# Nonlinear part of two chunks in joined operations, with one scale for w_out, in a kernel of sigmoid attention and an MLP

## The chip, the cores and the metric

The kernel runs on one core of a Trainium2 chip. The metric is the device time of one execution in microseconds. An engine's name stands for its queue too: instructions of one engine run in the order in which they stand, and an instruction that waits holds up all that stand behind it.

## The reference

Attention with a sigmoid in place of the softmax, over 8 batches of 12 heads, 448 positions and 64 values a head, then an MLP whose nonlinear function is made of three pieces.

```python
scores = scale * np.matmul(q, k.transpose(0, 1, 3, 2)) - np.log(S)
attn = 1.0 / (1.0 + np.exp(-scores))
x = np.matmul(attn, v)                      # (8, 12, 448, 64) -> (3584, 768)
h = x @ w_in                                # (3584, 2048)
g = np.where(h >= 1, h, np.where(h <= -1, 0.0, (h + 1) ** 2 / 4))
return g @ w_out                            # (3584, 768)
```

Inputs and result are float32. The kernel works with float16 pairs: a number is scaled by a power of two and split in a high and a low half, and a product of two numbers is three matmuls (high by high, high by low, low by high).

## The kernel before

**Batches.** The work goes batch by batch (b = 0 to 7), each with 448 columns. The attention of batch b + 1 (`scores`, `weigh`, `av`: lines 410 to 530) runs between the MLP matmuls of batch b. It comes in pieces: score matmuls into `psc` (L438, L429), a sigmoid on ScalarE (L474), its high half on ScalarE (L482) and low half on VectorE (L483), then matmuls with v into `pav` (L520).

**The MLP of a batch.** Its first half makes h, 2048 rows in 16 chunks of 128, and from it g, as float16 halves in `ghl[:, f, half, :]` for chunk f. Its second half, the *downs* (`down`, L784), makes 6 output tiles, each from 48 matmuls over the 16 chunks, and scales and stores them.

**Batches 0 and 1** make h chunk by chunk (`up`, L748) and apply the nonlinear part to each (`bend`, L753 to L765). w_out is split in two groups of 8 chunks, each with a scale of its own (`wo.scale[0]`, `wo.scale[1]`), since the first group is needed in batch 0 before all of w_out has been seen.

**Batches 2 to 7** work at half size (`up_blocks`, L697): h of chunks i and i + 8 together, a *pair*, is made from 7 products of half-size blocks (9 matmuls of 224 columns each, L714), with weights combined beforehand (`mix`) and stored as `blocks`. The products j = 0 to 6 of pair i add up in four quarters of PSUM, in two banks `hold[i, 0]` and `hold[i, 2]`. VectorE and ScalarE put the quarters together: `u2` and `u3` are partial sums, and the four quarters of the result are a copy of quarter 0 (L732) and three sums (L723), in `hf` (chunk i) and `hg` (chunk i + 8). Three PSUM banks are shared by products and downs, so a bank's sums must be read before products of the next pair but one can start. After the last product both chunks get their nonlinear part:

```python
nc.scalar.activation(g, h, AF.Relu, bias=hr, scale=ihr)                                              # L761
nc.vector.scalar_tensor_tensor(out=g, in0=g, scalar=rt, in1=g, op0=ALU.min, op1=ALU.mult)            # L762
nc.vector.scalar_tensor_tensor(out=g, in0=h, scalar=ihs, in1=g, op0=ALU.mult, op1=ALU.max)           # L763
latest["g"] = nc.scalar.activation(hi, g, AF.Copy)                                                   # L764
(nc.gpsimd if f % GPOOL else nc.vector).tensor_tensor(out=ghl[:, f, 1, :], in0=g, in1=hi, op=ALU.subtract)  # L765
```

`GPOOL` is 1, so L765 runs on VectorE. The scales (`hr`, `ihr`, `rt`, `ihs`) are one number per batch and group, worked out by one-column operations on VectorE (`small`, L578) in `common_scales`. There the groups' different w_out scales are met by square roots (`roots`, `wo.root`, `wo.iroot`): each group's g gets a scale that makes up for that of its w_out, so that the downs can add up both groups.

**Order.** A scheduler places the instructions of all engines by priorities and by its own estimate of times; the sums of quarters have a raised priority (`Q_PRIO`). Loads and stores are issued by SyncE in the order of the program. GpSimd splits q, k and v of later head pairs (L373 to L375) and copies corner blocks (L454).

Of the kernel before, what the change touches and what calls it, by code (L numbers as in the profile page):

```python
# [71 lines left out]
def sigmoid_attention_mlp(ctx: ExitStack, tc: tile.TileContext, first_qvk, qkv, w_in, w_out, out_t):  # L72
# [525 lines left out]
    def inverse(tag, s):  # L598

        return small(tag, s, -1.0, ALU.mult, float(2 * 127 * EXP_ONE), ALU.add, ints=True)  # L600
# [5 lines left out]
        up_sc[b, k] = sc = up_scales(*largest(inv_x, k), k)  # L606
        down_sc[b, k] = lambda: small("od%d" % k, inverse("ig%d" % k, sc[4]), wo.inv[k], ALU.mult)

    def roots():

        for k in range(2):
            for t, lst, n in ((wo.scale[k], wo.root, "root"), (wo.inv[k], wo.iroot, "iroot")):
                r = const.tile([P, 1], F32, name=n + str(k))
                nc.vector.tensor_scalar(
                    out=r.bitcast(I32), in0=t.bitcast(I32), scalar1=0.5, scalar2=float(127 * EXP_ONE // 2),
                    op0=ALU.mult, op1=ALU.add,
                )
                lst.append(r)
# [80 lines left out]
    def up_blocks(b, i, j):  # L699

        n = (b - SB) * (NFC // 2) + i
        if j % 2 == 0 and j < 4:
# [8 lines left out]
        out, w = quarter(q), sets[n % 3]
        for c in range(HC):
            for wh, xh in ((0, 0), (0, 1), (1, 0)):
                nc.tensor.matmul(  # L714
                    out, w[:, wt, wh, c * P : (c + 1) * P], xc[:, xt, c, xh, :],
                    start=j in (0, 2) and c + wh + xh == 0, stop=c == HC - 1 and wh == 1,
                    skip_group_check=True,
                )
# [4 lines left out]
        add = lambda out, q, other: nc.vector.tensor_tensor(out=out, in0=quarter(q), in1=other, op=ALU.add)  # L723
        with tc.high_priority(offset=Q_PRIO):
            if j == 1:
                nc.scalar.activation(u2, quarter(0), AF.Copy)
# [28 lines left out]
    def bend(b, f, h):  # L755

        ihr, hr, rt, ihs, _ = up_sc[b, int(f >= NA)]
        g = tmp_p.tile([P, S], F32, tag="tmp", name="g")
        hi = ghl[:, f, 0, :]

        nc.scalar.activation(g, h, AF.Relu, bias=hr, scale=ihr)  # L761
        nc.vector.scalar_tensor_tensor(out=g, in0=g, scalar=rt, in1=g, op0=ALU.min, op1=ALU.mult)  # L762
        nc.vector.scalar_tensor_tensor(out=g, in0=h, scalar=ihs, in1=g, op0=ALU.mult, op1=ALU.max)  # L763
        latest["g"] = nc.scalar.activation(hi, g, AF.Copy)  # L764
        (nc.gpsimd if f % GPOOL else nc.vector).tensor_tensor(out=ghl[:, f, 1, :], in0=g, in1=hi, op=ALU.subtract)  # L765
# [124 lines left out]
    for u, unit in enumerate(units):  # L890
# [12 lines left out]
        if wo.at < NA + 1:  # L903
            convert(wo, min(NA + 1, (u + 1) * (NA + 1) // WO_A))
            if wo.at == NA + 1:
                wo.find_scale()
                split_at = 0
        elif wo.at < NFC + 1:
            convert(wo, min(NFC + 1, NA + 1 + (u + 1 - WO_A) * (NFC - NA) // (WO_B - WO_A)))
            if wo.at == NFC + 1:  # L910
                wo.find_scale()
                roots()
        if len(wo.scale):
            while split_at < min(NA, 2 * (u + 1 - WO_A)):
# [85 lines left out]
```

## Time and profile before

| what | us |
|---|---|
| median of 3 runs (1158.22, 1158.45, 2932.11) | 1158.45 |
| profiled execution, its own time | 1152.84 |
| its span, first to last instruction | 1151.1 |
| idle TensorE in the span (1151.1 - 1120.0) | 31.1 |
| length of one half-size batch (499.75 to 636.43 us) | 136.7 |

The run of 2932.11 us is no typical one; the median stands on the other two. Batches 2 to 5 repeat with the same length. In a row of groups the columns are line, engine, operation, output and inputs, shape and count, then busy time and mean time of one, then idle time before it and what ended that. In a row of the timeline the first two numbers are start and length in us, and the brackets hold the idle time before and its releaser. In a row of waits stand the total in us, how often, and the longest.

### The profile page before, as it was taken

How to read it: one execution, taken by the hardware profiler on the slowest of the kernel's cores; microseconds unless marked ns; L12 is line 12 of the kernel's file. 1: busy time of each engine (PE TensorE's matmuls, PEld its weight loads, DVE VectorE, ACT ScalarE, POOL GpSimd, SP SyncE). 2: the span in 40 equal slices, each digit the busy share in tenths (PEclk: the TensorE clock that was granted, in tenths of full speed). 3: DMA queues.
4: the chain of work that ended last, by engine and by line, in shares of the span. 5: the costliest groups of instructions: out<-in, count | busy, mean ns of one | idle time of the engine just before them, and what ended most of it. 6: DMA issues, size and time to landing. Idle time of an engine off the chain costs nothing.

```text
span 1151.1 us, 20032 instructions
## 1 busy us (share of the span) xinstructions
PE 1120.0 (97%) x7914; PEld 660.7 (57%) x7914; DVE 831.4 (72%) x1730; ACT 721.2 (63%) x1199; POOL 291.3 (25%) x367
## 2 busy tenths in 40 slices
PE   8899999999889999999999999999999998999998
PEld 2234434444446775478645776457754677548954
DVE  6988977789985996469945798368974599646820
ACT  6978988679765785457754687347773476423410
POOL 0000000003442344323623353515344234110000
PEclk9999999999999999999999999999999999999999
DMA  9933432153453653125421345114532054103300
GB/s 367 394 107 132 162 124 74 35 192 119 161 182 120 220 193 108 49 91 193 157 105 50 130 170 195 50 50 169 186 140 69 22 189 173 65 17 123 136 24 25
DMA packets 32511, 151.64 MB, mean 132 GB/s; under 512 B 3488, under 2 KB 14240, under 8 KB 26272
## 3 DMA queue, kind: packets, MB, share of 16 engines
q1 hardware_dynamic: 30688, 140.92, 33.8%
q10 hardware_dynamic: 1728, 9.44, 2.2%
q8 instruction: 62, 1.02, 0.4%
q14 instruction: 33, 0.27, 0.1%
HBM read 126.94 MB, written 23.40 MB: 131 GB/s over the span
## 4 chain that ended last, share of the span: by engine, by line
PE 67%; DVE 20%; ACT 7%; issue 2%; DMA 2%; SPq 0%; DVEq 0%; ACTq 0%
PE po L784 35%; PE ph L714 11%; PE ph L748 8%; PE pav L520 6%; DVE ahl L483 5%; PE psc L438 4%; DVE g L762 4%; DVE g L763 3%; DVE xhl L723 2%; ACT ahl L482 2%; ACT psc L474 2%; DVE ghl L765 1%; PE psc L429 1%; DMA blocks<-mixs 1%; ACT ghl L764 1%
## 5 line engine op out<-in xcount | busy, mean ns | idle before, releaser
L784 PE MATMUL po<-ghl,w_out_sb 128*128 128x448 f16 x2304 | 447.7, 354 | 2.9 <-DVE g L763 2.9
L784 PEld LDWEIGHTS <-w_out_sb 128*128 128x128 f16 x2304 | 222.5, 98 | 220.4 <-issue 19.5
L714 PE MATMUL ph<-w_in_sb 128*128 128x224 f16 x3024 | 303.7, 259 | 10.6 <-DVE xhl L723 10.5
L714 PEld LDWEIGHTS <-w_in_sb 128*128 128x128 f16 x3024 | 284.4, 98 | 37.7 <-issue 36.4
L483 DVE SCALAR_TENSOR_TENSOR ahl<-psc,ahl 128x896 f16<-128x896 f32 (+1 forms) x170 | 153.0, 900 | 113.2 <-ACT ahl L482 111.4
L474 ACT ACTIVATE psc<-psc,nls,sqk 128x896 f32<-128x896 f32 (+1 forms) x136 | 130.3, 971 | 116.6 <-PE psc L438 113.4
L373 POOL TENSOR_SCALAR raw<-raw,qkv_s 128x448 f32<-128x448 f32 (+1 forms) x93 | 68.6, 752 | 427.6 <-DVE qkv_i L137 368.5
L482 ACT ACTIVATE ahl<-psc 128x896 f16<-128x896 f32 (+1 forms) x170 | 128.0, 762 | 23.3 <-DVE ahl L483 21.8
L748 PE MATMUL ph<-xhl,w_in_sb 128*128 128x448 f16 x576 | 112.8, 353 | 0.0
L761 ACT ACTIVATE g<-xhl,hr,ihr 128x448 f32<-128x448 f32 x96 | 67.8, 753 | 56.4 <-DVE xhl L723 56.2
L764 ACT ACTIVATE ghl<-g 128x448 f16<-128x448 f32 x128 | 73.2, 572 | 46.5 <-DVE g L763 46.4
L765 DVE TENSOR_TENSOR ghl<-g,ghl 128x448 f16<-128x448 f32 x128 | 91.1, 718 | 11.9 <-ACT ghl L764 11.0
L723 DVE TENSOR_TENSOR xhl<-ph,xhl 128x224 f32<-128x224 f32 x240 | 86.3, 382 | 16.9 <-PE ph L714 10.6
L762 DVE SCALAR_TENSOR_TENSOR g<-g,rk 128x448 f32<-128x448 f32 x112 | 83.9, 764 | 14.8 <-ACT g L761 14.3
L438 PE MATMUL psc<-hl 64*128 64x448 f16 x756 | 91.3, 352 | 0.3 <-ACT a L471 0.3
L748 PEld LDWEIGHTS <-w_in_sb 128*128 128x128 f16 x576 | 54.6, 98 | 59.9 <-issue 9.7
L520 PE MATMUL pav<-ahl,v 128*64 128x448 f16 x748 | 83.7, 357 | 0.0
L375 POOL TENSOR_TENSOR hl<-raw,hl 128x448 f16<-128x448 f32 x62 | 72.5, 1190 | 0.0
L797 DVE TENSOR_SCALAR o<-po,od 128x448 f32<-128x448 f32 x42 | 28.5, 679 | 59.0 <-PE po L784 58.8
L763 DVE SCALAR_TENSOR_TENSOR g<-xhl,ihs,g 128x448 f32<-128x448 f32 x96 | 69.3, 739 | 0.1
L337 ACT ACTIVATE dump<-raw 128x448 f16<-128x448 f32 (+1 forms) x105 | 61.5, 586 | 2.7 <-DVE mb L154 1.3
L454 POOL COPY w_in_sb<-hl 64x128 f16<-64x128 f16 x68 | 27.8, 409 | 129.3 <-DVE hl L369 127.4
(149 smaller groups left out, 1080.0 us busy)
## 6 DMA issues: line engine op xcount, KB each, us to landing
w_in_sb<-blocks SPq DMA_DIRECT2D x48, 1344.0 KB, 6.0
raw<-qkv SPq DMA_DIRECT2D x34, 704.0 KB, 4.2
w_out_sb<-w_in SPq DMA_DIRECT2D x16, 768.0 KB, 11.1
out_t<-o SPq DMA_DIRECT2D x48, 224.0 KB, 1.9
blocks<-mixs SPq DMA_DIRECT2D x8, 768.0 KB, 3.3
w_out_sb<-w_out ACTq DMA_DIRECT2D x6, 768.0 KB, 4.9
raww<-w_out ACTq DMA_DIRECT2D x6, 768.0 KB, 5.3
blocks<-mixp SPq DMA_DIRECT2D x8, 576.0 KB, 3.4
```

The source lines that it names most:

```text
L438: run(lambda: nc.tensor.matmul(out, hl[rows, 1, kh, w], hl[rows, 0, qh, :], start=t == 0, stop=t == 2))
L474: nc.scalar.activation(a, a, AF.Sigmoid, bias=nls, scale=sqk)
L482: nc.scalar.activation(hi, x, AF.Copy, scale=ATT)
L483: made.setdefault(i, []).append(nc.vector.scalar_tensor_tensor(out=lo, in0=x, scalar=ATT, in1=hi, op0=ALU.mult, op1=ALU.subtract))
L520: run(lambda: once(nc.tensor.matmul(pav[j * D : (j + 1) * D, :S], *terms[j][t], start=c == 0 and t == 0, stop=mid and t == len(terms[j]) - ...
L714: nc.tensor.matmul(out, w[:, wt, wh, c * P : (c + 1) * P], xc[:, xt, c, xh, :], start=j in (0, 2) and c + wh + xh == 0, stop=c == HC - 1 a ...
L723: add = lambda out, q, other: nc.vector.tensor_tensor(out=out, in0=quarter(q), in1=other, op=ALU.add)
L748: nc.tensor.matmul(ph[:, :S], w_in_sb[:, f, wh, c * P : (c + 1) * P], xhl[:, c, xh, :], start=c == 0 and wh + xh == 0, stop=c == NCC - 1 a ...
L762: nc.vector.scalar_tensor_tensor(out=g, in0=g, scalar=rt, in1=g, op0=ALU.min, op1=ALU.mult)
L763: nc.vector.scalar_tensor_tensor(out=g, in0=h, scalar=ihs, in1=g, op0=ALU.mult, op1=ALU.max)
L765: (nc.gpsimd if f % GPOOL else nc.vector).tensor_tensor(out=ghl[:, f, 1, :], in0=g, in1=hi, op=ALU.subtract)
L784: nc.tensor.matmul(po[:, :S], w_out_sb[:, f, wh, m * P : (m + 1) * P], ghl[:, f, gh, :], start=f == lo and wh + gh == 0, stop=f == hi - 1 ...
```

## The change

In batches 2 to 7 the nonlinear part of a pair is one chain of five operations over both chunks, 2 x 448 columns (`bends`), where there were two chains of five operations of 448. Its intermediate g no longer has a tile of its own: it lies, as float32, in the place in `ghl` where the halves of chunks i and i + 8 will stand. Two of the three sums of quarters (quarter 3 and quarter 2, each plus u2) become one operation of 2 x 224 columns.

One operation has one scale, so both groups of w_out must have one too. Once the second group's scale is known, `join_scales` takes the smaller of both; the second group is split with that, and the first group, split already, is multiplied by the ratio in batch 1 (`rescale`, eight GpSimd operations of 1536 columns, one for each chunk). `roots` goes, and `common_scales` gets shorter. Batches 0 and 1 keep `bend`.

```diff
-    def roots():
...
+    def join_scales():
+        for lst, n, op in ((wo.scale, "wos", ALU.min), (wo.inv, "woi", ALU.max)):
+            t = const.tile([P, 1], F32, name=n)
+            nc.vector.tensor_scalar(out=t, in0=lst[0], scalar1=lst[1], scalar2=None, op0=op)
+            lst[1] = t
+        wo.ratio = const.tile([P, 1], F32, name="wor")
+        nc.vector.tensor_scalar(out=wo.ratio, in0=wo.scale[1], scalar1=wo.inv[0], scalar2=None, op0=ALU.mult)
+
+    def rescale(f):
+        w = w_out_sb[:, f].rearrange("p h n -> p (h n)")
+        nc.gpsimd.tensor_scalar(out=w, in0=w, scalar1=wo.ratio, scalar2=1.0, op0=ALU.mult, op1=ALU.mult)
+
     def common_scales(b, inv_x, ih=None):
         big = [largest(inv_x, k) for k in range(2)]
-        q = [small("q%d" % k, big[k][1], wo.root[k], ALU.mult) for k in range(2)]
-        q = small("qm", q[0], q[1], ALU.min)
+        rt = small("rk", big[0][1], big[1][1], ALU.min)
         for k in range(2):
-            up_sc[b, k] = up_scales(ih or big[k][0], small("rk%d" % k, q, wo.iroot[k], ALU.mult), k)
-        od = inverse("od", small("qq", q, q, ALU.mult))
+            if k and ih:
+                up_sc[b, 1] = up_sc[b, 0]
+            else:
+                up_sc[b, k] = up_scales(ih or big[k][0], rt, k)
+        od = small("od", inverse("ig", up_sc[b, 0][4]), wo.inv[1], ALU.mult)
...
-                add(hg[:, :HN], 2, u2)
-                add(hf[:, HN:], 3, u2)
+                both = hold[i, 2].rearrange("p (k n) -> p k n", k=2)[:, ::-1, :HN]
+                nc.vector.tensor_tensor(
+                    out=h[:, HN : 3 * HN].rearrange("p (k n) -> p k n", k=2), in0=both,
+                    in1=u2.unsqueeze(1).to_broadcast([P, 2, HN]), op=ALU.add,
+                )
         if j == 6:
-            bend(b, i + NFC // 2, hg)
-            bend(b, i, hf)
+            bends(b, i, h.rearrange("p (k n) -> p k n", k=2))
...
+    def bends(b, i, h):
+        ihr, hr, rt, ihs, _ = up_sc[b, 0]
+        g = ghl.rearrange("p f h n -> p f (h n)").bitcast(F32)[:, i :: NFC // 2, :]
+        hi, lo = (ghl[:, i :: NFC // 2, t, :] for t in range(2))
+        nc.scalar.activation(g, h, AF.Relu, bias=hr, scale=ihr)
+        nc.vector.scalar_tensor_tensor(out=g, in0=g, scalar=rt, in1=g, op0=ALU.min, op1=ALU.mult)
+        nc.vector.scalar_tensor_tensor(out=h, in0=h, scalar=ihs, in1=g, op0=ALU.mult, op1=ALU.max)
+        nc.scalar.activation(hi, h, AF.Copy)
+        nc.vector.tensor_tensor(out=lo, in0=h, in1=hi, op=ALU.subtract)
...
         if b == 1:
             mix_scales()
+            for f in range(NA):
+                rescale(f)
```

The scheduler places the instructions anew. In the changed kernel the lines are L719 for the products, L728 and L740 for the sums, L780 to L784 for the five operations of `bends`, L803 for the downs and L621 for the rescale.

VectorE at the end of the products of the last batch, before: the last sums, then the operations of both chunks (`rk_11674` and `rk_11664`, `ihs_11678` and `ihs_11668` are the scales of the two groups).

```order
L723 TENSOR_TENSOR xhl<-ph,xhl 128x224
L762 SCALAR_TENSOR_TENSOR g<-g,rk_11664 128x448
L763 SCALAR_TENSOR_TENSOR g<-xhl,ihs_11678,g 128x448
L763 SCALAR_TENSOR_TENSOR g<-xhl,ihs_11668,g 128x448
L765 TENSOR_TENSOR ghl<-g,ghl 128x448 x2
L723 TENSOR_TENSOR xhl<-ph,xhl 128x224 x2
L762 SCALAR_TENSOR_TENSOR g<-g,rk_11674 128x448
L762 SCALAR_TENSOR_TENSOR g<-g,rk_11664 128x448
```

And with the change: from the two sums of the last pair (L728) on, L781 and L782 are those of pair 6, L740 the joined sum of pair 7, L784 the difference of pair 6, and the last row the first operation of pair 7.

```order
L728 TENSOR_TENSOR xhl<-ph,xhl 128x224 x2
L781 SCALAR_TENSOR_TENSOR ghl<-ghl,rk 128x2x448
L782 SCALAR_TENSOR_TENSOR xhl<-xhl,ihs_11260,ghl 128x896
L740 TENSOR_TENSOR xhl<-ph,xhl 128x448
L784 TENSOR_TENSOR ghl<-xhl,ghl 128x2x448
L781 SCALAR_TENSOR_TENSOR ghl<-ghl,rk 128x2x448
```

Before, the differences of pair 6 (L765) stood ahead of the last sums; now that of pair 6 (L784) stands behind the last sum, since the copy that it reads ends later. In the built program the Relu of pair 7 also waits for this difference: both touch `ghl` in a range that reaches from chunk i to chunk i + 8.

TensorE at the same place, before (with buffer numbers; `ph_12375` is a bank of pair 7, `po_12438` the first output tile, `po_12490` the second; rows left out repeat the row above or load weights):

```order
L714 MATMUL ph_12312<-w_in_sb_90 128x224
...
L784 MATMUL po_12438<-ghl_94,w_out_sb_91 128x448
...
L714 MATMUL ph_12375<-w_in_sb_90 128x224
...
L784 MATMUL po_12438<-ghl_94,w_out_sb_91 128x448
...
L784 MATMUL po_12490<-ghl_94,w_out_sb_91 128x448
```

And with the change (`ph_11901` and `ph_11846` belong to pair 7, `po_11956`, `po_12008` and `po_12060` are the first three output tiles):

```order
L719 MATMUL ph_11846<-w_in_sb_90 128x224
...
L803 MATMUL po_11956<-ghl_94,w_out_sb_91 128x448
...
L719 MATMUL ph_11901<-w_in_sb_90 128x224
...
L803 MATMUL po_12008<-ghl_94,w_out_sb_91 128x448
...
L803 MATMUL po_12060<-ghl_94,w_out_sb_91 128x448
...
L803 MATMUL po_11956<-ghl_94,w_out_sb_91 128x448
```

Before, 22 downs of the first tile stood ahead of the last 18 products, and 20 more of it behind them before the tile needed chunk 7. Now 3 stand ahead, and 3 of the second and 3 of the third tile behind; the next, the first tile with chunk 8, waits in the built program for the first VectorE operation of pair 7 (L781), whose range in `ghl` reaches over chunk 8. In batches 2 to 6 the same change stands there, with attention matmuls in between.

GpSimd, around the new operations (w_out_sb<-w_out_sb,wor is the rescale):

```order
L147 AFFINE_SELECT ident<-ident 128x128
L451 MEMSET w_in_sb 128x256 x2
L621 TENSOR_SCALAR w_out_sb<-w_out_sb,wor 128x1536 x8
L454 COPY w_in_sb<-hl 64x2x64 x6
L373 TENSOR_SCALAR raw<-raw,qkv_s 128x448 x2
L373 TENSOR_SCALAR raw<-raw,qkv_s 128x512
```

Otherwise GpSimd's order is as before, and SyncE's is the same.

More of the change, by code (lines that the diff above doesn't have):

```diff
@@ L607, in group_scales @@
         down_sc[b, k] = lambda: small("od%d" % k, inverse("ig%d" % k, sc[4]), wo.inv[k], ALU.mult)
-    def roots():
[L611 to L618, printed above, removed]
+    def join_scales():
[8 more added lines that the diff above has]
+        nc.gpsimd.tensor_scalar(out=w, in0=w, scalar1=wo.ratio, scalar2=1.0, op0=ALU.mult, op1=ALU.mult)
     def common_scales(b, inv_x, ih=None):
         big = [largest(inv_x, k) for k in range(2)]
-        q = [small("q%d" % k, big[k][1], wo.root[k], ALU.mult) for k in range(2)]
-        q = small("qm", q[0], q[1], ALU.min)
+        rt = small("rk", big[0][1], big[1][1], ALU.min)
         for k in range(2):
-            up_sc[b, k] = up_scales(ih or big[k][0], small("rk%d" % k, q, wo.iroot[k], ALU.mult), k)
-        od = inverse("od", small("qq", q, q, ALU.mult))
+            if k and ih:
[3 more added lines that the diff above has]
+        od = small("od", inverse("ig", up_sc[b, 0][4]), wo.inv[1], ALU.mult)
         down_sc[b, None] = lambda: od
@@ L718, in up_blocks @@
                 )
-        hf, hg = (rows[:, (i % 2 * 2 + k) * S : (i % 2 * 2 + k + 1) * S] for k in range(2))
+        h = rows[:, i % 2 * 2 * S : (i % 2 + 1) * 2 * S]
         u2, u3 = (rows[:, 4 * S + i % 2 * S + k * HN : 4 * S + i % 2 * S + (k + 1) * HN] for k in range(2))
@@ L729, in up_blocks @@
                 add(u3, 2, u2)
-                add(hg[:, HN:], 3, u3)
+                add(h[:, 3 * HN :], 3, u3)
             elif j == 4:
-                nc.scalar.activation(hf[:, :HN], quarter(0), AF.Copy)
+                nc.scalar.activation(h[:, :HN], quarter(0), AF.Copy)
             elif j == 6:
-                add(hg[:, :HN], 2, u2)
-                add(hf[:, HN:], 3, u2)
+                both = hold[i, 2].rearrange("p (k n) -> p k n", k=2)[:, ::-1, :HN]
[3 more added lines that the diff above has]
+                )
         if j == 6:
-            bend(b, i + NFC // 2, hg)
-            bend(b, i, hf)
+            bends(b, i, h.rearrange("p (k n) -> p k n", k=2))
     hold = {}
@@ L848, in sigmoid_attention_mlp @@
     wo = Weight(w_out, w_out_sb, "wo", [13, 15, 9, 11, 13, 15, 9, 11, 0, 0, 13, 15, 0, 0, 0, 0])
-    wo.root, wo.iroot = [], []
     at = 0
@@ L911, in sigmoid_attention_mlp @@
                 wo.find_scale()
-                roots()
+                join_scales()
         if len(wo.scale):
```

## The prediction

> **What bounds the kernel now.** I read the page's head and chain first, then what TensorE (PE) waited for, then stretches of one batch, then single operations.
>
> ```profile
> span 1151.1 us, 20032 instructions
> PE 1120.0 (97%) x7914; PEld 660.7 (57%) x7914; DVE 831.4 (72%) x1730; ACT 721.2 (63%) x1199; POOL 291.3 (25%) x367
> ...
> PE 67%; DVE 20%; ACT 7%; issue 2%; DMA 2%; SPq 0%; DVEq 0%; ACTq 0%
> ```
>
> TensorE is busy 1120.0 of 1151.1 us, so whatever happens to the other engines, only 31.1 us of idle TensorE can be won. The waits of TensorE for other engines are these:
>
> ```profile
> PE ph L714 <- DVE xhl L723: 10.5, 6, 3.2
> PE psc L425 <- DMA ghl<-first_qvk: 4.3, 1, 4.3
> PE psc L425 <- ACT a L471: 3.5, 5, 1.3
> PE psc L173 <- DVE diag L163: 3.2, 1, 3.2
> PE po L784 <- DVE g L763: 2.9, 1, 2.9
> PE psc L429 <- DVE ahl L483: 1.4, 4, 0.3
> ```
>
> The first and the last row lie in the half-size batches (2 to 7): six waits for a quarter's sum (L723), which frees the PSUM bank of the products, and four for an attention remainder. Together 10.5 + 1.4 = 11.9 us: this is all that the change can take away. The rest lies in batches 0 and 1, which keep their chunk-wise nonlinear part. The two halves of batch 3, products and then downs:
>
> ```profile
> 499.75:565.27 65.52, 63.50 (x623) 51.34 (x625) 57.46 (x120) 49.93 (x88) 27.49 (x36) 1.00 0.46 165
> 565.27:636.43 71.16, 71.16 (x437) 36.21 (x438) 40.70 (x94) 36.61 (x65) 26.10 (x34) 1.00 0.23 85
> ```
>
> Columns after the length are busy PE, PEld, DVE, ACT, POOL. Where the nonlinear part runs, VectorE is 88% busy and TensorE lacks 2.02 us; in the downs TensorE never waits. The 2.02 us come late in the products:
>
> ```profile
> 549.29 0.74 PE L438 MATMUL psc<-hl 64*128 64x448 f16 x6
> 551.71 1.88 PE L714 MATMUL ph<-w_in_sb 128*128 128x224 f16 x18 [1.68 <-DVE xhl L723]
> 553.93 0.73 PE L429 MATMUL psc<-hl,w_in_sb 128*128 128x448 f16 x3 [0.34 <-DVE ahl L483]
> 554.59 1.33 PE L520 MATMUL pav<-ahl,v 128*64 128x448 f16 x12
> ```
>
> VectorE's queue has fallen behind by about 2 us when TensorE needs its next bank.
>
> **The joined operations.** Prices from batch 7, where no GpSimd work disturbs (first seven rows), and wider forms elsewhere:
>
> ```profile
> L723 DVE TENSOR_TENSOR xhl<-ph,xhl 128x224 f32<-128x224 f32 x38 | 13.9, 386 | 11.0 <-PE ph L714 8.1 <-ACT xhl L726 2.7
> L762 DVE SCALAR_TENSOR_TENSOR g<-g,rk 128x448 f32<-128x448 f32 x14 | 9.4, 679 | 1.7 <-ACT g L761 1.7
> L765 DVE TENSOR_TENSOR ghl<-g,ghl 128x448 f16<-128x448 f32 x14 | 8.5, 618 | 0.1
> L761 ACT ACTIVATE g<-xhl,hr,ihr 128x448 f32<-128x448 f32 x14 | 10.0, 752 | 13.1 <-DVE xhl L723 13.1
> L764 ACT ACTIVATE ghl<-g 128x448 f16<-128x448 f32 x14 | 8.1, 575 | 6.3 <-DVE g L763 6.3
> 1079.37 1.27 DVE L762 SCALAR_TENSOR_TENSOR g<-g,rk 128x448 f32<-128x448 f32 x2
> 1083.60 1.41 ACT L761 ACTIVATE g<-xhl,hr,ihr 128x448 f32<-128x448 f32 x2 [1.16 <-DVE xhl L723]
> ...
> L483 DVE SCALAR_TENSOR_TENSOR ahl<-psc,ahl 128x896 f16<-128x896 f32 x102 | 110.6, 1085 | 104.9 <-ACT ahl L482 104.8
> L282 DVE SCALAR_TENSOR_TENSOR w_out_sb<-w_out_sb,wo_s 128x768 f16<-128x768 f32 x16 | 16.2, 1013 | 2.2 <-ACT w_out_sb L279 2.0
> L474 ACT ACTIVATE psc<-psc,nls,sqk 128x896 f32<-128x896 f32 x102 | 107.6, 1065 | 113.6 <-PE psc L438 113.4
> L474 ACT ACTIVATE psc<-psc,nls,sqk 128x448 f32<-128x448 f32 x34 | 23.5, 691 | 3.0 <-PE psc L157 3.0
> ```
>
> VectorE: from 448 columns (679 ns) to 768 (1013) is 1.04 ns a column, so 896 columns take about 1.15 us; two of 448 in a row take 1.27. Each joined operation saves 0.12 us, three a pair 0.36, and the joined sum (386 + 224 x 1.04 = 0.62 against 0.69 for two that overlap like those above) 0.07: 0.43 us a pair, 3.4 a batch of 8, 21 us over 48 pairs. ScalarE: (1065 - 691) / 448 = 0.83 ns a column, so Relu takes 752 + 374 = 1.13 us (two: 1.41) and the copy 0.95 (two: about 1.15): 0.5 us a pair, 23 us in all. Nothing of this is on the path by itself; it counts only as far as it shortens the 11.9 us. The Trainium skill ("VectorE: DVE Perf Modes", section "The TRN2 errata — SBUF-src ops pay a fixed extra latency per instruction") gives an fp32 tensor_tensor (N + 151) / 0.96 ns: 624 at 448 columns, where the trace has 618, and as an estimate 1091 at 896, so that joining would save 0.16 us; the trace's queued pair shows that part of the fixed cost is overlapped already, and the sum takes 0.12.
>
> **The small scales.** For one batch 23 one-column operations become 15 (two q, qm, one rk, qq and the second four scales go, od gains one). At some 0.2 us (L578 rows have 144 to 209 ns) 1.6 us of VectorE per batch go, in the downs, where TensorE waits for nothing: worth 0. Three one-column operations at the joining take the place of four for the roots, ahead of the splits of the second half of w_out: +0 there. No DMA is added or moved; SyncE's order is the same.
>
> **The rescale.** Eight GpSimd operations of 1536 columns in batch 1, placed ahead of the first corner copy.
>
> ```profile
> L375 POOL TENSOR_TENSOR hl<-raw,hl 128x448 f16<-128x448 f32 x62 | 72.5, 1190 | 0.0
> L373 POOL TENSOR_SCALAR raw<-raw,qkv_s 128x448 f32<-128x448 f32 x62 | 44.2, 723 | 427.6 <-DVE qkv_i L137 368.5 <-issue 46.8 <-ACT dump L337 12.3
> L373 POOL TENSOR_SCALAR raw<-raw,qkv_s 128x512 f32<-128x512 f32 x31 | 25.1, 810 | 0.0
> 212.91 1.01 POOL L454 COPY w_in_sb<-hl 64x128 f16<-64x128 f16 x2 [82.69 <-DVE hl L369]
> 188.90:220.50 31.60, 31.60 (x169) 15.28 (x169) 26.87 (x62) 20.86 (x32) 0.95 (x2) 1.00 0.10 31
> L429 PE MATMUL psc<-hl,w_in_sb x3: 352/352/353, 243.8 to 244.2; 128*128 128x448 f16 x3
> ```
>
> The same operation costs (810 - 723) / 64 = 1.36 ns a column, so 2.2 us each and 18 us together; at the rate of L375 (1190 / 448 = 2.66) it would be 4.1 and 33. I take 18, as the same kind. They may begin when the first downs have read the weights, about 189 us, and end at 207, or 222 at worst: the corner copies of 212.91 then shift by up to 9 us, and TensorE reads them from 243.8 (L429). Their cover is an idle GpSimd and those 30 us; without it the attention of batch 1 would slip by 9. Worth 0, between 0 and +3. What speaks against it is the shared memory side:
>
> ```profile
> L762 DVE SCALAR_TENSOR_TENSOR g<-g,rk 128x448 f32<-128x448 f32 x12 | 9.9, 850 | 0.9 <-ACT g L761 0.9
> ```
>
> That is batch 3's row, with GpSimd at work: 850 ns against 679. Under the rescale VectorE may be 25% slower for 18 us, at most 4.5 us, where it has 31.60 - 26.87 = 4.73 us of slack. The Trainium skill ("GPSIMD Engine Reference", section "Key points") says that GpSimd shares its SBUF interfaces with VectorE and contends with instructions of two SBUF inputs; the trace agrees (850 against 679), and by it the rescale would cost TensorE nothing while that slack lasts.
>
> **The longer chain.** Before, a pair's two chunks overlap, one on ScalarE while the other is on VectorE. Now a pair is one chain: sum 0.62, Relu 1.13, two operations of 1.15, copy 0.95, difference 1.08 (618 + 448 x 1.04): 6.1 us. Two new waits come with it, since the intermediate now lies in ghl and spans chunks i to i+8: the Relu of a pair stands behind the difference of the pair before, and the downs' second chunk (8) stands behind the last pair's first VectorE operation. Batch 7 before:
>
> ```profile
> 1043.63 24.31 PE L714 MATMUL ph<-w_in_sb 128*128 128x224 f16 x252
> 1068.64 22.59 PE L714 MATMUL ph<-w_in_sb 128*128 128x224 f16 x234 [0.70 <-DVE xhl L723]
> 1091.06 4.33 PE L784 MATMUL po<-ghl,w_out_sb 128*128 128x448 f16 x22
> 1095.22 1.89 PE L714 MATMUL ph<-w_in_sb 128*128 128x224 f16 x18
> ```
>
> A pair has 63 products of 96.5 ns, 6.08 us. From the Relu of a pair to that of the next stand 1.13 + 1.15 + 0.33 (a sum of the next pair between) + 1.15 + 0.95 + 1.08 = 5.8 us: it just fits, with no wait inside batch 7. At its end TensorE has six down products after the last 18, 1.2 us. In that time VectorE does the last sum, then the difference of pair 6, then ScalarE the Relu, then VectorE the first operation. Counted from the end of pair 6's last product: its sum to 0.65, the difference of pair 5 to 1.75, Relu to 2.9, two operations to 5.2, copy to 6.2 (the last sum beside it), difference to 7.3, the last Relu to 8.4, its first operation to 9.6. TensorE after 45 products (4.3) and nine downs (1.8) stands there at 6.1 and waits 3.5. Before, 22 downs stood ahead of the last 18 and the wait there was nothing. Batch 7: +3.5, and the 0.70 goes: +2.8, between 0 and +5.
>
> In batches 2 to 6 attention products stand behind the last 18: three L429, twelve L520 and six L438 (0.7 + 1.3 + 0.7) and six downs (1.2), 3.8 us. Against it VectorE has the sum 0.6, an operation of attention 1.09 (L483, 1085 ns above), the pair's own 1.15, and between them a sum of 672 columns for the next batch and a cast, which I estimate at 1.2 together (672 x 1.04 ns and one short operation): 4.1. So 0.3 us a batch. I take 0.7 us for what is left of the 2.02: the load falls by 3.4 us, more than the wait, but VectorE now idles during each Relu (0.6 us a pair where nothing else is ready), up to 4.8 a batch, more than it saves. Ends: 0 and 4.
>
> **The sum.** Waits before: 2.0 in batches 2 to 5, 3.2 in batch 6, 0.7 in batch 7, 11.9 in all. After: five times 1.0 and 3.5, 8.5. The difference is -3.4 us: 1152.84 of the profiled execution becomes 1149.4. The median of the three runs, 1158.45, lies 5.6 above that execution; against it I say 1155.0.
>
> **Rivals.** (a) All waits of the half-size batches vanish: -11.9 us, 1146.5. For it: the load saved (3.4) exceeds the wait (2.02) everywhere; against: the chain. (b) Waits move instead of going: the order rather than the load makes them, 2 us a batch stay, and the ends add 0.3 x 5 and 2.8; with 1 to 3 us more a batch for Relus held behind differences 1160 to 1175. (c) Slower by over 2%: the chain sets the pace. A pair of batch 3 has 65.52 / 8 = 8.2 us. Alone it needs 5.8; the attention operations queued into it, rows of batch 3, lengthen it by up to 16.9 / 8 = 2.1 us on VectorE and (14.2 + 12.7) / 8 = 3.4 on ScalarE.
>
> ```profile
> L483 DVE SCALAR_TENSOR_TENSOR ahl<-psc,ahl 128x896 f16<-128x896 f32 (+1 forms) x19 | 16.9, 892 | 6.9 <-ACT ahl L482 6.7
> L482 ACT ACTIVATE ahl<-psc 128x896 f16<-128x896 f32 (+1 forms) x19 | 14.2, 754 | 1.6 <-DVE ahl L483 1.4
> L474 ACT ACTIVATE psc<-psc,nls,sqk 128x896 f32<-128x896 f32 (+1 forms) x13 | 12.7, 981 | 0.9 <-PE psc L438 0.5 <-PE psc L157 0.3
> ```
>
> Every us over 8.2 costs 8 x 5 = 40 us; from 8.8 us on it decides: 1182, and at 9.2 it is 1198. Against it: VectorE works off much of that while ScalarE copies.
>
> **How the numbers follow.** The forecast (1149 to 1159) 0.50, (a) 0.20, (b) 0.21, (c) 0.07, and a gain beyond all that can be seen 0.02. Two per cent, 23 us, is about what a measurement of this kernel can tell from no change: faster 0.02, within 0.91, slower 0.07. The range runs from (a) with its spread, 1145, into (b), 1168; it leaves out about 2 in 10.
>
> **What would show it.** Right: the wait of products for quarter sums falls from 10.5 to about 4 us, a wait of downs for the first joined operation appears, near 3.5 us at the last batch and under 1 elsewhere, joined VectorE rows near 1.15 us (1.3 beside GpSimd), and rescales near 2.2 us with no wait behind them. Wrong: a ScalarE row in batches 2 to 6 that waits for the difference for several us a batch, or TensorE under 62 us busy in a products stretch longer than 66.

## The result, and the profile after

The changed kernel takes 1187.01 us (median of 4 runs, 1185.53 to 1188.82) beside 1158.34 us (median of 4) for the kernel before on the same chip. The ratio, which leaves the one run of 2932.11 us out, is 1.0257, 95% interval 1.0231 to 1.0282: slower by 2.6%, where the prediction said 1155.0 and 1145 to 1168.

The page of the changed kernel, in the parts that answer to those of before (the last five rows are groups: busy time, mean ns of one, then the idle time before them and what ended it):

```profile
span 1185.5 us, 19674 instructions
PE 1128.8 (95%) x7914; PEld 665.4 (56%) x7914; DVE 791.4 (67%) x1485; ACT 703.0 (59%) x1103; POOL 319.0 (27%) x375
...
PE 57%; DVE 17%; DMA 7%; POOL 7%; ACT 6%; issue 5%; SPq 0%; POOLq 0%; ACTq 0%; DVEq 0%
...
L337 ACT ACTIVATE dump<-raw 128x448 f16<-128x448 f32 (+1 forms) x105 | 61.5, 586 | 29.9 <-DMA raw<-qkv 27.6
L780 ACT ACTIVATE ghl<-xhl,hr,ihr 128x896 f32<-128x896 f32 x48 | 54.4, 1134 | 39.0 <-DVE xhl L740 28.4
L783 ACT ACTIVATE ghl<-xhl 128x896 f16<-128x896 f32 x48 | 45.6, 949 | 45.6 <-DVE xhl L782 45.2
L781 DVE SCALAR_TENSOR_TENSOR ghl<-ghl,rk 128x896 f32<-128x896 f32 x48 | 59.1, 1232 | 16.8 <-ACT ghl L780 16.8
L784 DVE TENSOR_TENSOR ghl<-xhl,ghl 128x896 f16<-128x896 f32 x48 | 55.8, 1162 | 8.9 <-ACT ghl L783 8.9
```

VectorE has 40 us less to do than before (831.4) and ScalarE 18 less (721.2), and yet the span is 34.4 us longer. The chain that ended last now has 7% DMA and 7% GpSimd in it, where before it had 2% DMA and no GpSimd. L337 is a line that the diff doesn't touch: on ScalarE it takes the absolute maximum of a q, k or v that has just been loaded. It now waits 27.6 us for those loads, 6.2 to 7.9 us of them in each of batches 2 to 5. In the kernel before ScalarE waits for no load at L337 at all, as the row of its page shows:

```profile
L337 ACT ACTIVATE dump<-raw 128x448 f16<-128x448 f32 (+1 forms) x105 | 61.5, 586 | 2.7 <-DVE mb L154 1.3
```

What TensorE waits for, in the changed kernel (total, how often, longest):

```profile
PE ph L719 <- DVE xhl L728: 11.4, 13, 1.2
PE psc L438 <- DVE ahl L483: 8.7, 8, 1.5
...
PE ph L719 <- DVE xhl L740: 4.8, 9, 1.3
PE po L803 <- DVE ghl L781: 4.3, 4, 3.2
```

Products waiting for quarter sums: 16.2 us instead of 10.5. Attention matmuls waiting for L483: 8.7 us. The downs waiting for the first joined operation: 4.3 us, 3.2 of it in batch 7.

The products of batch 3, from the first to the end of the last, in the view by stretches (length, then busy PE, PEld, DVE, ACT, POOL), in the kernel before and in the changed one:

```profile
499.68:571.68 72.00, 69.98 (x675) 55.89 (x674) 63.87 (x129) 55.94 (x100) 33.90 (x41) 1.00 0.46 165
...
511.37:585.47 74.10, 68.88 (x670) 55.56 (x669) 57.08 (x103) 54.78 (x88) 34.48 (x41) 1.00 0.45 161
```

TensorE idles 5.22 us in the second and 2.02 in the first; VectorE, 89% busy before, is at 77%, and ScalarE, 78% before, at 74%: neither has too much work. (The stretch of 65.52 us in the prediction ends before the last 27 products.)

How one such wait comes about, in batch 3, from the timeline of the changed kernel (start, length, engine, operation; in brackets the idle time before and its releaser):

```profile
561.32 2.00 POOL L375 TENSOR_TENSOR v<-raw,v 128x512 f16<-128x512 f32 x1
...
563.35 0.33 SPq L321 DMA_DIRECT2D raw<-qkv  x1
...
567.53 0.58 ACT L337 ACTIVATE dump<-raw 128x448 f16<-128x448 f32 x1 [2.27 <-DMA raw<-qkv]
568.01 0.19 ACT L337 ACTIVATION_READ_ACCUMULATOR dump<-raw 128x1 f32 x1
568.10 1.05 ACT L474 ACTIVATE psc<-psc,nls,sqk 128x896 f32<-128x896 f32 x1
...
569.64 0.90 ACT L482 ACTIVATE ahl<-psc 128x896 f16<-128x896 f32 x1
...
570.58 1.09 DVE L483 SCALAR_TENSOR_TENSOR ahl<-psc,ahl 128x896 f16<-128x896 f32 x1 [3.17 <-ACT ahl L482]
571.59 0.38 DVE L728 TENSOR_TENSOR xhl<-ph,xhl 128x224 f32<-128x224 f32 x1
...
572.02 1.89 PE L719 MATMUL ph<-w_in_sb 128*128 128x224 f16 x18 [1.23 <-DVE xhl L728]
```

Read downwards: GpSimd finishes with a raw buffer at 563.32; at 563.35 SyncE can issue the next load into it; ScalarE, which has the maximum of that load next in its queue, stands still until 567.53. Behind it stand the sigmoid (L474) and the high half (L482) of an attention piece. VectorE idles 3.17 us for that high half, does L483, and only then the quarter sum (L728), for which TensorE has waited 1.23 us. Nothing of this is in the joined operations themselves.

### The profile page after: what moved, and what is told of

The parts are those of the page before. It is cut to its first block, busy times and chain, and to the rows that moved or that the text cites. A ratio compares the mean times of both kernels' runs of the same rounds, so it can differ in the third digit from the quotient of the medians.

```text
span 1185.5 us, 19674 instructions
## 1 busy us (share of the span) xinstructions
PE 1128.8 (95%) x7914; PEld 665.4 (56%) x7914; DVE 791.4 (67%) x1485; ACT 703.0 (59%) x1103; POOL 319.0 (27%) x375
## 4 chain that ended last, share of the span: by engine, by line
PE 57%; DVE 17%; DMA 7%; POOL 7%; ACT 6%; issue 5%; SPq 0%; POOLq 0%; ACTq 0%; DVEq 0%
PE po L803 33%; PE ph L755 8%; PE ph L719 5%; PE pav L520 5%; DMA raw<-qkv 4%; DVE ahl L483 4%; PE psc L438 3%; DVE ghl L781 2%; POOL hl L375 2%; POOL raw L373 2%; DVE xhl L782 2%; ACT psc L474 1%; PE psc L425 1%; ACT ahl L482 1%; POOL v L375 1%
## 5 line engine op out<-in xcount | busy, mean ns | idle before, releaser
L803 PE MATMUL po<-ghl,w_out_sb 128*128 128x448 f16 x2304 | 450.7, 355 | 8.3 <-DVE ghl L781 4.3
L803 PEld LDWEIGHTS <-w_out_sb 128*128 128x128 f16 x2304 | 222.7, 98 | 228.9 <-issue 29.5
L719 PE MATMUL ph<-w_in_sb 128*128 128x224 f16 x3024 | 307.3, 261 | 16.2 <-DVE xhl L728 11.4
L719 PEld LDWEIGHTS <-w_in_sb 128*128 128x128 f16 x3024 | 287.0, 98 | 45.0 <-issue 42.6
L483 DVE SCALAR_TENSOR_TENSOR ahl<-psc,ahl 128x896 f16<-128x896 f32 (+1 forms) x170 | 152.8, 899 | 136.9 <-ACT ahl L482 135.7
L474 ACT ACTIVATE psc<-psc,nls,sqk 128x896 f32<-128x896 f32 (+1 forms) x136 | 129.9, 969 | 146.6 <-PE psc L438 144.9
L373 POOL TENSOR_SCALAR raw<-raw,qkv_s 128x448 f32<-128x448 f32 (+1 forms) x93 | 80.5, 879 | 436.5 <-DVE qkv_i L137 344.0
L482 ACT ACTIVATE ahl<-psc 128x896 f16<-128x896 f32 (+1 forms) x170 | 127.9, 762 | 17.5 <-DVE ahl L483 15.8
L755 PE MATMUL ph<-xhl,w_in_sb 128*128 128x448 f16 x576 | 113.6, 353 | 1.8 <-DVE xhl L544 1.7
L337 ACT ACTIVATE dump<-raw 128x448 f16<-128x448 f32 (+1 forms) x105 | 61.5, 586 | 29.9 <-DMA raw<-qkv 27.6
L780 ACT ACTIVATE ghl<-xhl,hr,ihr 128x896 f32<-128x896 f32 x48 | 54.4, 1134 | 39.0 <-DVE xhl L740 28.4
L783 ACT ACTIVATE ghl<-xhl 128x896 f16<-128x896 f32 x48 | 45.6, 949 | 45.6 <-DVE xhl L782 45.2
L781 DVE SCALAR_TENSOR_TENSOR ghl<-ghl,rk 128x896 f32<-128x896 f32 x48 | 59.1, 1232 | 16.8 <-ACT ghl L780 16.8
L375 POOL TENSOR_TENSOR hl<-raw,hl 128x448 f16<-128x448 f32 x62 | 67.0, 1100 | 0.0
L784 DVE TENSOR_TENSOR ghl<-xhl,ghl 128x896 f16<-128x896 f32 x48 | 55.8, 1162 | 8.9 <-ACT ghl L783 8.9
L438 PEld LDWEIGHTS <-hl 64*128 64x128 f16 x756 | 28.8, 95 | 58.3 <-issue 32.4
L728 DVE TENSOR_TENSOR xhl<-ph,xhl 128x224 f32<-128x224 f32 x144 | 55.2, 384 | 8.4 <-ACT xhl L731 6.1
L520 PEld LDWEIGHTS <-v 128*64 128x64 f16 x748 | 36.6, 110 | 37.1 <-issue 18.9
```

Of the source, the lines that this page charges most:

```text
L337: ins = nc.scalar.activation(dump[:, : rt.shape[1]], rt, AF.Abs, accum_out=m[:, t : t + 1])
L373: nc.gpsimd.tensor_scalar(out=rt, in0=rt, scalar1=s[:, t : t + 1], scalar2=1.0, op0=ALU.mult, op1=ALU.mult)
L375: nc.gpsimd.tensor_tensor(out=dst[:, 1, :], in0=rt, in1=hi, op=ALU.subtract)
L438: run(lambda: nc.tensor.matmul(out, hl[rows, 1, kh, w], hl[rows, 0, qh, :], start=t == 0, stop=t == 2))
L474: nc.scalar.activation(a, a, AF.Sigmoid, bias=nls, scale=sqk)
L482: nc.scalar.activation(hi, x, AF.Copy, scale=ATT)
```

## The experiments

Every kernel was timed beside the kernel before on the same chip, so the ratios are what to compare. The table cuts one profiled execution of each into stretches, in us; the ends are the start of the matmul L173 for the scale of batch 1 (185.5 us before), the start of the first product of each half-size batch, and the last instruction.

| kernel | ratio to before (95%) | to batch 1 | batch 1 | batches 2-5 | batch 6 | batch 7 |
|---|---|---|---|---|---|---|
| before | 1 | 185.5 | 177.5 | 546.7 | 133.9 | 107.5 |
| after | 1.0257 (1.0231-1.0282) | 187.6 | 181.5 | 569.0 | 134.3 | 113.0 |
| 1 two chains again | 1.0061 (1.0039-1.0082) | 185.7 | 181.8 | 549.8 | 134.2 | 106.8 |
| 2 own tile | 1.0205 (1.0176-1.0235) | 185.5 | 183.6 | 566.0 | 132.3 | 108.6 |
| 3 maxima in order | 1.0214 (1.0189-1.0239) | 190.7 | 182.9 | 554.0 | 136.9 | 114.4 |
| 4 no rescale | 1.0239 (1.0208-1.0269) | 187.7 | 180.0 | 566.7 | 136.7 | 113.6 |
| 5 maxima in order, late | 1.0173 (1.0158-1.0188) | 186.8 | 179.4 | 557.3 | 135.7 | 114.0 |
| 6 = 5 + 2 | 0.9998 (0.9984-1.0011) | 185.2 | 178.3 | 547.8 | 132.2 | 108.9 |
| 7 before, free dump | 1.0319 (1.0298-1.0340) | 187.0 | 175.0 | 580.2 | 140.6 | 107.5 |
| 8 = 6, rescales spread | 0.9986 (0.9973-0.9998) | 186.5 | 178.8 | 547.8 | 132.2 | 109.2 |
| 9 = 5 + tile for last pair | 0.9968 (0.9951-0.9985) | 185.5 | 178.1 | 546.3 | 132.2 | 106.7 |
| 10 before, maxima in order | 1.0086 (1.0054-1.0119) | 186.6 | 174.3 | 557.5 | 136.5 | 107.6 |
| 11 = 5 + two chains | 1.0063 (1.0041-1.0085) | 185.6 | 178.0 | 554.4 | 134.9 | 106.6 |
| 12 = 6, no rescale | 0.9958 (0.9940-0.9976) | 187.0 | 176.0 | 547.9 | 132.2 | 108.6 |

So of the 34.4 us, 22.3 lie in batches 2 to 5, 5.5 in batch 7, 4.0 in batch 1, 2.2 in the start, and 0.4 in batch 6, in which no L337 waits for a load. The start of the changed kernel's trace holds 3.4 us at half clock (from 59.5 us), that of the kernel before none; such spells, of 3.4 or 6.8 us, stand in most of the traces, so that differences of 1 to 3 us between single stretches say little.

**1. Two chains again.** Which part of the change costs the time?

```diff
-            bends(b, i, h.rearrange("p (k n) -> p k n", k=2))
+            bend(b, i + NFC // 2, h[:, S:])
+            bend(b, i, h[:, :S])
```

> The changed kernel with the nonlinear part of a half-size batch done chunk by chunk again, twice 448 columns with the intermediate in a tile of its own; common scale, rescale and joined sum stay. If the joined chain (the long operations, the intermediate in ghl, or what they do to the order of ScalarE's queue) costs the time: about 1162 us, the 22 us of batches 2 to 5 and the 5 of batch 7 gone, the 4 of batch 1 still there. If the joined sum or the common scales were the cause: 1183 or more, as in the changed kernel.

1162.4 us, ratio 1.0061. Batches 2 to 5 lose 3.1 us instead of 22.3 and batch 7 nothing; batch 1 keeps its loss, 4.3 us. The joined sum, the common scales and the rescale are not the main cause: `bends` is, or what comes with it. L337 waits for no load here either.

**2. Own tile.** The intermediate in a buffer (`raww`) that lies free from batch 2 on.

```diff
-        g = ghl.rearrange("p f h n -> p f (h n)").bitcast(F32)[:, i :: NFC // 2, :]
+        g = raw_p.tile([P, 2 * DM], I32, tag="raww", name="g").bitcast(F32)[:, : 2 * S].rearrange("p (k n) -> p k n", k=2)
```

> The changed kernel with the intermediate of a pair in a tile of its own (two buffers that lie free from batch 2 on) in place of ghl's bytes, so that a Relu no longer stands behind the difference of the pair before, and the downs' chunk 8 no longer behind the last pair's first VectorE operation. Theory chain (these two waits cost the time): 1160 to 1172 us. Theory order (ScalarE's queue has the absolute maxima of the next q, k, v ahead of their loads): batches 2 to 5 stay, only the wait at the ends goes, 1180 to 1184.

1179.47 us, close to the 1180 to 1184 of the theory of the order. Batch 7 gets 4.4 us of its 5.5 back, batches 2 to 5 only 3.0 of 22.3. One row of what ScalarE waits for, and one of what TensorE waits for:

```profile
ACT dump L337 <- DMA raw<-qkv: 45.6, 17, 7.6
```

```profile
PE po L803 <- ACT ghl L783: 11.2, 4, 2.8
```

ScalarE now stands at L337 for 45.6 us, not 27.6, and the ends of batches 2 to 5 wait for the last pair's copy (L783), 2.8 us each.

**3. Maxima in order.** L337 is held on ScalarE in the order of the program's text, which the kernel before does for the first pairs only.

```diff
-                    if p < NFULL + 3:
-                        tc.keep_in_program_order(ins)
+                    tc.keep_in_program_order(ins)
```

> The changed kernel with the absolute maxima (L337) held on ScalarE in the order of the program's text, one group of three per step instead of groups put ahead early by the scheduler; the joined operations are unchanged. Theory order: the 27.6 us in which L337 waits for a DMA fall below 8 and the time to 1162 to 1175 us. Theory chain: the DMA wait may go, but Relu and copy still wait, and the time stays at 1183 to 1190.

1180.44 us: between the two. L337 waits for no load any more, and batches 2 to 5 get 15.0 of their 22.3 us back. But the start and batch 1 lose 4.4 us more than in the changed kernel, and batches 6 and 7 lose 4.0; I took it that the held order doesn't suit batches 0 and 1, which wasn't shown; run 5 holds L337 later.

**4. No rescale.** The eight operations on GpSimd are left out, so that the first eight chunks of w_out keep a scale that the downs don't undo.

```diff
-            for f in range(NA):
-                rescale(f)
```

> The changed kernel without the eight rescales of w_out's first half on GpSimd (the first eight chunks of w_out keep a scale of their own that the downs of batches 1 to 7 don't undo). Theory contention (VectorE is slowed to half speed under them and batch 1 slips): -4 us, about 1183, with L544 near 0.7 us instead of 1.8 at 185 to 201 us. Rival (they are hidden, batch 1's 4 us come from elsewhere): 1186 to 1188.

1182.71 us, 1.0239; the interval overlaps that of the changed kernel, so the time alone doesn't decide. The trace does. L544 makes the low halves of batch 1's x on VectorE; here is its row for the changed kernel (ns: least, median, most), with the rescales beside it:

```profile
L544 DVE SCALAR_TENSOR_TENSOR xhl<-x,x_s,xhl x12: 672/680/1898, 68.6 to 201.0; 128x448 f16<-128x448 f32 x12
...
184.88 15.73 POOL L621 TENSOR_SCALAR w_out_sb<-w_out_sb,wor 128x1536 f16<-128x1536 f16 x8 [52.48 <-DVE od L578]
```

and for the kernel without them:

```profile
L544 DVE SCALAR_TENSOR_TENSOR xhl<-x,x_s,xhl x12: 672/674/684, 68.7 to 194.4; 128x448 f16<-128x448 f32 x12
```

Under the rescale an L544 takes up to 1898 ns instead of 674, and the last of batch 1's six starts 6.6 us later. Between 183 and 215 us TensorE waits 1.7 us for L544 and 1.4 for a sigmoid; without the rescale 0.5 in all. That is 2.6 us.

**5. Maxima in order, late.** As 3, but from pair 18 on.

```diff
-                    if p < NFULL + 3:
+                    if p < NFULL + 3 or p >= 18:
```

> The changed kernel with the absolute maxima held in the order of the text from pair 18 on only, so that batches 0 and 1 keep the changed kernel's order. From the profile of the run that held them from the start: batches 2 to 5 at 138.5 us instead of 142.3 (15 us less), batch 1 as in the changed kernel, about 1171 us. If holding them gains nothing where it doesn't also cost in batches 0 and 1: 1180 or more.

1175.36 us, 4 above what was expected. Batches 2 to 5 are at 557.3, 11.7 below the changed kernel and 10.6 above before, and batch 7 is at 114.0. The waits of TensorE from 1050 us on:

```profile
PE po L803 <- DVE ghl L781: 3.2, 1, 3.2
PE po L803 <- DVE xhl L740: 0.9, 1, 0.9
```

The first row is the wait of the downs' second chunk for the last pair's first operation; the second stands ahead of it, and L740 is the sum that reads the last pair's bank. Both are there in batches 2 to 5 as well. In the whole run they are

```profile
PE po L803 <- DVE ghl L781: 5.5, 6, 3.2
PE po L803 <- DVE xhl L740: 3.7, 5, 1.0
```

9.2 us, 5.1 of them in batches 2 to 5.

**6. Both.** 5 and 2 together.

> Both: absolute maxima in the order of the text from pair 18 on, and the intermediate in a tile of its own. If the two causes add (order 15 us, the two waits behind ghl's bytes 1.8 us a batch and 4 at the end): 1160 to 1164 us, batches 2 to 5 at 136.7 to 137.2. If the tile gives nothing once the order is mended, because the rest is ScalarE's time in long operations itself: 1168 to 1172.

1155.82 us, ratio 0.9998: all of the loss is gone, below what was expected. The two edits gave 0.8% and 0.5% alone and 2.6% together. Part of that is the clock: the mean granted clock of 5 and then of 6,

```profile
core 0: 1173.2 us, clock 0.990
```

```profile
core 0: 1152.4 us, clock 0.996
```

At 0.990, 11.7 us of the span's full clock are missing, at 0.996 4.6. With the 9.2 us of waits that is 16 of the 20.8 us between the two spans; what the rest is wasn't followed.

**7. Before, with a free dump.** The output of L337 that nobody reads (`dump`) lies, in both kernels, in one of the three `tmp` buffers, which in the kernel before the chunks' g use too. `bends` needs no `tmp` buffer. My theory was now that this is what sets L337 free to go ahead. So the kernel before, with its chunk-wise operations and without any part of the change, gets one edit:

```diff
-                    dump = tmp_p.tile([P, S], F32, tag="tmp", name="dump").bitcast(F16)
+                    dump = raw_p.tile([P, 2 * DM], I32, tag="raww", name="dump").bitcast(F16)
```

> The kernel before, with one edit: the unused output of the absolute maxima lies in a buffer of its own instead of one of the three that the chunks' intermediates use. With that the scheduler puts the maxima early, in front of their loads, as in the changed kernel. Theory order: even with the operations of 448 columns ScalarE is held by the loads (L337 waiting for a DMA over 15 us in all) and the time rises to 1164 to 1176. Theory that only long operations make the order matter: within 3 us of before, 1154 to 1160.

1193.05 us, ratio 1.0319: slower than the changed kernel, and beyond the 1164 to 1176 that were expected. Its page:

```profile
L337 ACT ACTIVATE dump<-raw 128x448 f16<-128x448 f32 (+1 forms) x105 | 62.0, 591 | 82.3 <-DMA raw<-qkv 72.8
```

and what its TensorE waits for:

```profile
PE ph L714 <- DVE xhl L723: 17.4, 12, 3.3
PE ph L714 <- ACT xhl L732: 11.3, 5, 3.1
```

The scheduler, no longer held back by a buffer, puts L337 ahead of its load; ScalarE stands there for 72.8 us, and batches 2 to 5 lose 33.5 us. No joined operation is needed for the loss.

**8. Rescales spread.** 6, with the rescales one by one through batch 1, held in the order of the text on GpSimd.

```diff
-            for f in range(NA):
-                rescale(f)
...
+                    if u % 9 == 0 and u < 9 * NA:
+                        rescale(u // 9)
```

> The two edits together and the rescales spread in the order of the text over batch 1 instead of eight in a row. If the contention comes from their closeness, 2 to 3 us less than without spreading, 1158 to 1162; if each costs VectorE the same wherever it stands, no difference to the run without it.

1154.68 us. The intervals of 6 and 8 overlap, and batch 1 has 178.8 us beside 178.3: no difference shown. In the built order four of the eight still stand together, so that this says little on closeness.

**9. Tile for the last pair alone.** 5, with one more edit; the other seven pairs keep their intermediate in `ghl`.

```diff
+        if i == NFC // 2 - 1:
+            g = raw_p.tile([P, 2 * DM], I32, tag="raww", name="g").bitcast(F32)[:, : 2 * S].rearrange("p (k n) -> p k n", k=2)
```

> As the run with the absolute maxima late, but the last pair of a batch alone has its intermediate in a tile of its own; seven of eight Relus still stand behind the difference of the pair before. If the downs' wait at a batch's end is the rest (3.2 us in batch 7, about 1.5 in batches 2 to 5, and the clock halved behind it): 1154 to 1160 us. If it is the Relu held behind the difference: 1167 or more.

1152.75 us, 1 below what was expected, ratio 0.9968: faster than before by 0.3%, 3.7 us, and the lowest ratio of all that compute the whole result (the interval overlaps that of 8). Its page, and batch 3's products in the view by stretches:

```profile
span 1148.9 us, 19686 instructions
...
PE 1119.2 (97%) x7914; PEld 661.5 (58%) x7914; DVE 799.9 (70%) x1485; ACT 704.3 (61%) x1103; POOL 317.9 (28%) x375
...
L337 ACT ACTIVATE dump<-raw 128x448 f16<-128x448 f32 (+1 forms) x105 | 61.5, 586 | 2.5 <-DVE mb L154 1.3
```

```profile
500.08:570.65 70.57, 68.43 (x671) 55.11 (x668) 58.43 (x103) 54.28 (x90) 34.13 (x41) 1.00 0.46 169
```

Seven of eight Relus still stand behind the difference of the pair before, and batches 2 to 5 are at 546.3, as before. So with L337 held those waits cost nothing, and what the place of g costs lies at the end of a batch: 11.0 us in batches 2 to 5 between 5 and 9, 7.3 in batch 7. Why 9 is ahead of 6 was not tried; of the 3.5 us between their spans a spell of half clock in batch 2 of 6 makes 1.6, and 2.2 lie in batch 7.

**10. Before, maxima in order**, the edit of 5 on the kernel before.

> The kernel before with the absolute maxima held in the order of the text from pair 18 on. Its own order left 2 us of waits a batch, so 1150 to 1158 us: the difference to the joined kernel with the same two orders says what the change is worth once the order is held. If this comes under 1150, the order of the kernel before was not as good as its waits made it look.

1166.32 us, above what was expected: the held order is worse for the chunk-wise kernel than its own, by 0.9%, with 19.3 us of products waiting for quarter sums (L723).

**11. Two chains, maxima in order**, the edits of 1 and 5.

> The changed kernel with the nonlinear part chunk by chunk and the absolute maxima in the order of the text: what the joining alone is worth, beside the run that has both joining and tile (1155.8). Joining worth what I priced (about 1 us a batch of waits): 1157 to 1162. Joining worth nothing: 1154 to 1157.

1163.15 us, 1 above what was expected. With the same hold on L337, 9 has the joined operations and is 0.95% faster (0.9968 against 1.0063), in every one of batches 2 to 6. But in 11 the chunks' g and the output of L337 still share the three `tmp` buffers, and in 9 they don't. Chunk-wise operations with L337 held and its output elsewhere were not tried, so that how much of the 0.95% is due to the joining isn't shown.

**12. Order, tile, no rescale**, the edits of 6 and 4, with the same part of w_out left at a scale that isn't undone.

> The run with order and tile, without the eight rescales (the first eight chunks of w_out keep a scale that the downs don't undo). If they cost in batch 1 what they did in the changed kernel: 3 us less, 1152 to 1154. If that kernel's batch 1 has slack for them: 1155 to 1157.

1150.67 us, ratio 0.9958, 0.4% below 6 and below what was expected. Batch 1 is 2.3 us shorter (176.0 against 178.3), all else the same within 0.3 but the start. So the rescale costs some 2.5 us in batch 1, by the length of the batch in 12 and 6 and by TensorE's waits in 4 and the changed kernel. (Batch 1 of 4 is only 1.5 us shorter than that of the changed kernel, but 6.8 us more of it ran at half clock.) The medians of 6 and 12 say 5, and what the rest is stays open.

## Why the prediction was wrong, point by point

**The step that failed** is the one on batches 2 to 6. "I take 0.7 us for what is left of the 2.02" and "So 0.3 us a batch" for the ends made 1.0 us of waits a batch, 1.0 less than before; in the trace each of batches 2 to 5 is 5.0 to 6.1 us longer than before.

The first term weighed the load of VectorE, its idle time and the two new waits written into the chain. What it left out is that the change also takes a tenant away: without g, only L337 and, once a batch, a small diagonal (L162) ask for a `tmp` buffer in batches 2 to 7. The old tenant's hold on it had kept L337 behind its load. The text compared the orders of VectorE, TensorE and GpSimd and named SyncE's as unchanged; ScalarE's queue it left out. Run 7 (the edit that frees the buffer, alone, +3.2%) shows that this is enough for such a loss; runs 3 and 5, in which L337 is held and nothing else is changed, give back 15.0 and 11.7 of the 22.3 us in batches 2 to 5.

The second term, the ends, was too small: in batches 2 to 5 run 5 takes 11.0 us more than run 9, 2.8 a batch where 0.3 was said. 5.1 of them are waits of the downs for L781 and L740, and two spells of half clock make up to 3.4. The two causes don't simply add up. Moving g alone (2) gives back only 3.0 us of the 22.3, for there ScalarE stands still for loads for 45.6 us and not 27.6; with both mended (6 and 9) batches 2 to 5 lose at most 1.1 us.

**Two readings** in the prediction were off. Its stretch of 65.52 us for batch 3's products ends before the last 27 of them; up to the last it is 72.00, so that a pair had 9.0 us and not 8.2, and the 8.8 of rival (c) would not have gone beyond it. And at the ends 0.7, 1.3, 0.7 and 1.2 make 3.9, not 3.8, and the terms against them 4.0, not 4.1: 0.1 us and not 0.3.

**Rival (c)** gave the right time, 1182 to 1198, by the wrong mechanism. Run 9 keeps the chain, its durations and seven of its eight waits, and is faster than before. Neither of the two signs that the prediction gave for being wrong appeared as written: in batches 2 to 6 ScalarE doesn't wait for the difference but for a DMA (in batch 7 it waits for the difference, 7.0 us in six waits, but TensorE is busy for 49.25 of the 49.29 us up to the last products), and TensorE is busy 68.88 of 74.10 us in the longer products stretch, not under 62. The signs named for being right failed with the first of them: the wait of products for quarter sums rose to 16.2 us and did not fall to 4.

**Right, by the rows above.** Relu 1134 ns (1.13 said), copy 949 (0.95), first operation 1232 (1.15 to 1.3), difference 1162 (1.08, without GpSimd beside it). The rescales take 1.97 us each (2.2). Nothing speaks for a cost of the small scales. With L337 held and g moved, the joined operations do no harm: run 6 is level with the kernel before, and run 9 is 3.7 us faster, close to the 3.4 us that were forecast; since it has two edits more than the change that was forecast, that is luck. Whether the joining is worth more, run 11 leaves open.

**Batch 7**: +3.5 for the wait of chunk 8 said, and 0.70 saved; the timeline of the changed kernel shows

```profile
1123.26 0.73 PE L803 MATMUL po<-ghl,w_out_sb 128*128 128x448 f16 x3 [0.90 <-DVE xhl L740]
1127.19 8.09 PE L803 MATMUL po<-ghl,w_out_sb 128*128 128x448 f16 x33 [3.20 <-DVE ghl L781]
```

3.20 there and 0.90 ahead of it; the 0.70 of before, which stood among the products, is gone. The 5.5 us of the batch, 0.5 beyond my upper end, hold one thing more: the 33 downs behind the wait take 8.09 us, 1.6 more than 33 at the 197 ns of the prediction's row of 22, since in their first 3.4 us half the clock was granted (the row of the stretch from 1127.90 us stands in the last section).

**The rescale**: the price of one was right, "VectorE may be 25% slower" was not. The row that I took it from (850 against 679 ns) is a mean over twelve operations in a stretch in which GpSimd was busy for less than half of the time (27.49 of 65.52 us); under an unbroken run of f16 operations L544 is slowed by a factor of up to 2.8. The cost of 2.5 us is inside my 0 to +3 by luck, not by the reasoning: the last L544 came 6.6 us later, more than the 4.73 us of slack that I had counted on. The Trainium skill ("GPSIMD Engine Reference", section "Key points") names contention of GpSimd with VectorE instructions of two SBUF inputs; L544 is one, and the trace agrees, with this factor.

**Batch 1's other 1.5 us** (4.0 less 2.5) were not followed; in run 9, which has the rescales too, batch 1 is at 178.1, 3.4 below the changed kernel. **Batch 6** was to get 2.2 us shorter and is 0.4 longer; in runs 6 and 9 it is 1.7 shorter.

## What to carry to other kernels

Freeing a buffer is not free of consequences where a scheduler orders the queues: whatever shared the buffer may now be placed earlier, and in a queue that runs in order, as ScalarE's does here, an instruction placed ahead of its load stops everything behind it. So ask of each tile that a change gives up who else uses its slots, and compare the order on every engine, above all on those whose own instructions hardly change. And in this kernel's framework a tile written in strides is taken by its whole range: an intermediate put in a result's place makes its readers wait for it; here, with L337 held, it was enough to give the last one a place of its own.

## What the runs showed of the hardware that I had not expected

TensorE's clock was halved by stalls that add up, not only by one long one. The timeline of the changed kernel's TensorE in batches 2 and 3:

```profile
440.07 0.74 PE L438 MATMUL psc<-hl 64*128 64x448 f16 x6 [1.47 <-DVE ahl L483]
441.63 3.36 PE L719 MATMUL ph<-w_in_sb 128*128 128x224 f16 x18 [0.82 <-DVE xhl L728]
...
582.02 0.74 PE L438 MATMUL psc<-hl 64*128 64x448 f16 x6 [1.46 <-DVE ahl L483]
583.59 1.89 PE L719 MATMUL ph<-w_in_sb 128*128 128x224 f16 x18 [0.82 <-DVE xhl L728]
```

and two stretches by themselves, in batch 2 and in batch 7 (the third number from the end is the granted clock):

```profile
441.80:445.20 3.40, 3.40 (x20) 2.54 (x19) 3.06 (x4) 2.34 (x3) 3.40 (x3) 0.50 0.00 0
...
1127.90:1131.30 3.40, 3.40 (x11) 1.37 (x9) 1.52 (x2) 0.95 (x1) 0.00 (x0) 0.50 0.00 0
```

In batch 2, idle times of 1.47 and 0.82 us, 2.29 of the 3.03 us from the start of the first to the end of the second, are followed by 3.4 us at half clock, and the same 18 products take 3.36 us instead of 1.89. In batch 3 the same two stalls are not.

The traces of all fourteen kernels say when. In each, the clock changes only on a grid of steps of 3.413 us. Cut into windows on that grid, from 60 to 1140 us, they show this of TensorE at full clock: each of the 30 windows in which it was busy for less than 40% was followed by one at half clock, 11 of the 48 with 40 to 55% were, and none of the 4288 with more. In batch 2 both stalls lie in one window, busy for 33%; in batch 3 the edge between two windows, at 581.75 us, cuts the first stall, and they are busy for 65 and 69%.

The Trainium skill ("TensorE: Matmul & The Clock Gate", "Part 1") puts the fall to half clock after at least one idle window of some 3.4 us and calls the window free-running; the length of the spell and the chance in where it falls agree, but here TensorE had worked for about a third of a window of that length (3.4 less 2.29 us). So short stalls that fall together in one window, some 2 us in all, can cost up to 1.7 us (half of 3.4) more than their own length.
